# Second weights split one unit ahead, a pass edge's high parts before the weight splits, balancing sums in another bank: windowed attention and a Sinkhorn-balanced mixture of experts on one core

## The chip, the core and the metric

The program runs on one core of a Trainium2 chip. Its engines each work through a queue of their own in order: PE (matrix multiply, with PEld for its weight loads), DVE, ACT and POOL (elementwise), SP (which here issues the DMAs). Semaphores order the queues against each other. The metric is the device time of one execution in microseconds (us); lower is better.

## The reference, cut to what matters

```python
scores = scale * q @ k.T                     # batch 4, heads 8, seq 576, head_dim 64
scores = where(0 <= i - j < 64, scores, -1e9)
x = (softmax(scores) @ v) as [N=2304, D=512]
P = exp(x @ w_gate - max)                    # E = 8 experts
for _ in range(8):
    P /= P.sum(1, keepdims=True) + 1e-9
    P /= P.sum(0, keepdims=True) + 1e-9
    P *= N / E
out = sum_e P[:, e] * (relu(x @ w1[e]) @ w2[e])   # w1[e]: 512x1024, w2[e]: 1024x512
```

## The kernel before

**Numbers in two parts.** Every matrix operand is held as a high part (a cast to a shorter float, made by ACT) and a low part (what the cast lost, a subtraction by POOL or DVE). A product of two operands is three matmuls: high by high, high by low, low by high.

**Stage 1** (to about 206 us of the span) computes attention for 18 tiles of 128 rows, the gate, and the first half of expert 0's work. What later passes need goes to DRAM (`xd_r`, `xd_f`, `yd`).

**Stage 2** runs three passes over 6 row tiles each (`NPASS`, `TP`). A pass has 30 groups: a group is 256 of an expert's 1024 inner columns; expert 0 has two groups left, the others four. Two groups make a unit, so a pass has 15 units and stage 2 has 45; units are numbered u0 to u44 here. In a unit, `Group.run` is called for the even and the odd group: seven products of half size (a Strassen scheme) of 12 column blocks' worth of `x` parts `xc[0..6]` with first-weight parts `w1c`, into PSUM banks `a`, `b` and `c` (two buffers each), with ACT and DVE making the two parts `g` of the relu. Then `mm2(u, t)` for t = 0..5 multiplies `g` by the second weights' parts `w2c` (12 matmuls into a PSUM tile `yp`, two buffers), and DVE adds the tile into `acc`, scaled by the balanced probability. The first unit of an expert that opens a new sum has ACT work here too: `L252` scales `acc` (u3, u16, u31), or `L247` copies `yp` away (u1).

**Weights.** `fetch1(i)` and `fetch2(i)` load 512 KB of a group's first or second weights into one of three staging buffers `stg` (SP queue). `sums1` (POOL, 4 operations) makes the Strassen sums of the first weights; `split1` makes `w1c` (ACT casts at L143, POOL subtractions at L146); `split2` makes two `w2c` tiles (ACT casts at L155, POOL subtractions at L156). The ring of `w2c` has eight tiles, four per unit. Before the change `split2(s)` and `split2(s + 1)` stand in the same unit whose `mm2` reads them, at a hook (`extra(k)`) inside the even and the odd group.

**Balancing.** Eight Sinkhorn rounds run as `step()` after `mm2` tiles 0, 2 and 4 of u0 and u1 and 0 and 2 of u2: a matmul with the constant `part` gives column sums (L680) in a buffer of the ring `y`, the ring of `yp`, and DVE rescales `prob` (L682 to L684, L674 to L676). `sk_exp` before u0 puts the maximum in such a buffer and has ACT take the exponential (L670).

**Pass edges.** u14 and u29 end a pass. Shortly before, three units of each of the first two passes (u10 to u12, u25 to u27) load attention output for the next pass (`xd_f`) and form its four Strassen sums on POOL (`next_sums`, L266 to L269), behind the even group. In the edge unit `next_slot` reloads `xc[0..2]` by DMA and makes `xc[3..6]` from these sums: a cast on ACT (L707) and a subtraction on DVE (L708) after each of `mm2` tiles 0 to 3. `split1(s + 3)` stands after tile 1.

The order on every engine is the order of the code (`tc.manual_schedule`): no scheduler moves anything.

Of the kernel before, what the change touches and what calls it, by code (L numbers as in the profile page):

```python
# [11 lines left out]
ALU = mybir.AluOpType  # L12
# [9 lines left out]
def window_attention_sinkhorn_moe(ctx: ExitStack, tc: tile.TileContext, q, k, v, w_gate, w1, w2, out):  # L22
    nc = tc.nc
# [39 lines left out]
    xc = [big.tile([P, 2, 2, NB], F32R, name=f"xc{i}") for i in range(7)]  # L63
# [6 lines left out]
    def f32(ap):  # L70
        return ap.bitcast(F32)
# [33 lines left out]
    def fetch1(i):  # L105
        if i < len(groups):
            _, e, c = groups[i]
            stg = r_stg.new()
            nc.sync.dma_start(out=stg, in_=w1[e, :, c * 2 * P:(c + 1) * 2 * P].rearrange("(k p) f -> p k f", p=P))
            raw1[i] = stg  # L110

    def fetch2(i):
        if i < len(groups):
            _, e, c = groups[i]
            stg = r_stg.new().rearrange("p k f -> p (k f)").rearrange("p (c d) -> p c d", c=2)
            nc.sync.dma_start(out=stg, in_=w2[e, c * 2 * P:(c + 1) * 2 * P, :].rearrange("(c p) d -> p c d", p=P))
            raw2[i] = stg
# [14 lines left out]
    def split1(i):  # L132
        if i >= len(groups):
            return
        a, ws = raw1.pop(i), wsum.pop(i)
        w = r_w1.new()
        parts = [
            (slice(0, 2), a[:, 0:4, 0:P]),
            (slice(2, 3), a[:, 2:4, P:]),
            (slice(3, 7), ws.rearrange("p s k f -> p (s k) f")),  # L140
        ]
        for sl, src in parts:
            nc.scalar.copy(out=w[:, 0, sl].rearrange("p s k f -> p (s k) f"), in_=src)  # L143
        for sl, src in parts:
            o, h = (w[:, j, sl].rearrange("p s k f -> p (s k) f") for j in (1, 0))
            nc.gpsimd.tensor_tensor(out=o, in0=src, in1=f32(h), op=ALU.subtract)  # L146
        wt1[i] = w

    def split2(i):
        if i >= len(groups):  # L150
            return
        src = raw2.pop(i)
        for j in range(2):
            w = r_w2.new()
            nc.scalar.copy(out=w[:, 0], in_=src[:, j])  # L155
            nc.gpsimd.tensor_tensor(out=w[:, 1], in0=src[:, j], in1=f32(w[:, 0]), op=ALU.subtract)  # L156
            wt2[i, j] = w
# [4 lines left out]
    ps = {}  # L162
# [59 lines left out]
    side = {}  # L222
# [64 lines left out]
    with tc.manual_schedule():  # L287
# [348 lines left out]
        with ExitStack() as p2:  # L636
            ring_b = p2.enter_context(tc.tile_pool(name="ring_b", bufs=1, reuse_waits="tile"))
            sk_p = p2.enter_context(tc.tile_pool(name="sk", bufs=2, reuse_waits="tile"))
            ps_m = p2.enter_context(tc.tile_pool(name="ps_m", bufs=2, space=PSUM, reuse_waits="tile"))
            for nm in "abc":  # L640
                ps[nm] = lambda nm=nm: ps_m.tile([P, 512], F32, tag=f"q{nm}", name=f"q{nm}")[:, :NB]
            ps["y"] = lambda: ps_m.tile([P, 512], F32, tag="y", name="yp2")
            for r in rings.values():
                r.open(ring_b)

            def side_tile():
                return ring_b.tile([P, 4 * 2 * NB], F32, tag="side", name="side")

            side["acc"] = side_tile().rearrange("p (t d) -> p t d", t=TP)
            split1(1)  # L650
            fetch2(1)
            fetch1(2)


            pending = []
            state = {}

            def sk_tile(shape, name):
                n = 1
                for x in shape[1:]:  # L660
                    n *= x
                t = ps["y"]()[:shape[0], :n]
                return t.rearrange("p (t e) -> p t e", e=shape[2]) if len(shape) == 3 else t

            def sk_exp():
                mp = sk_tile([P, 1], "mb")
                nc.tensor.matmul(mp, lhsT=ones[0:1, :], rhs=max2, start=True, stop=True)
                nm = sk_p.tile([P, 1], F32, tag="nm", name="nm2", bufs=1)
                nc.vector.tensor_copy(out=nm, in_=mp)
                nc.scalar.activation(out=pv, in_=logit, func=AF.Exp, bias=nm)  # L670

            def sk_row():
                r = sk_p.tile([P, T], F32, tag="r", name="r")
                nc.vector.tensor_reduce(out=r, in_=prob[:, 0:T, :], axis=AX.X, op=ALU.add)  # L674
                nc.vector.reciprocal(out=r, in_=r)
                nc.vector.tensor_tensor(out=pv, in0=pv, in1=r[:, :, None].to_broadcast([P, T, E]), op=ALU.mult)  # L676

            def sk_col():
                cp = sk_tile([P, T + 1, E + 1], "cp")
                nc.tensor.matmul(cp, lhsT=part, rhs=prob, start=True, stop=True)  # L680
                c = sk_p.tile([P, E], F32, tag="c", name="c")
                nc.vector.tensor_reduce(out=c, in_=cp[:, :, 0:E].rearrange("p t e -> p e t"), axis=AX.X, op=ALU.add)  # L682
                nc.vector.reciprocal(out=c, in_=c)
                nc.vector.tensor_tensor(out=pv, in0=pv, in1=c[:, None, :].to_broadcast([P, T, E]), op=ALU.mult)  # L684

            sk_exp()
            sk_row()
            pending += [lambda: (sk_col(), sk_row())] * (ITERS - 1) + [sk_col]

            def step():  # L690
                if pending:
                    pending.pop(0)()


            def next_sums(p, j):
                if j == 0:
                    side["xt"] = side_tile().rearrange("p (i k n) -> p i k n", i=4, k=2)
                x = ring_b.tile([P, KD, 2 * P], F32, tag="xr2", name="xr2")
                nc.sync.dma_start(out=x, in_=xd_f[p - 1][j])
                x_sums(side["xt"][:, :, :, j * P:(j + 1) * P], x, nc.gpsimd)  # L700

            def next_slot(p, slot):
                if slot < 3:
                    nc.sync.dma_start(out=f32(xc[slot]), in_=xd_r[p - 1][:, slot])
                else:
                    src = side["xt"][:, slot - 3]
                    nc.scalar.copy(out=xc[slot][:, 0], in_=src)  # L707
                    nc.vector.tensor_tensor(out=xc[slot][:, 1], in0=src, in1=f32(xc[slot][:, 0]), op=ALU.subtract)  # L708

            n_units = len(groups) // 2  # L710
            per = n_units // NPASS
            for u in range(n_units):
                pas, at = divmod(u, per)
                more = pas + 1 < NPASS
                s = 2 * u

                def even(k):
                    if k == 1:
                        split2(s)
                        fetch1(s + 3)  # L720
                    elif k == 3 and more and per - 5 <= at < per - 5 + TP // 2:
                        next_sums(pas + 1, at - (per - 5))

                def odd(k):
                    if k == 0:
                        sums1(s + 2)
                        if more and at == per - 1:
                            next_slot(pas + 1, 0)
                    elif k == 1:
                        if more and at == per - 1:  # L730
                            next_slot(pas + 1, 1)
                        split2(s + 1)
                        fetch2(s + 2)
                    elif k == 3 and more and at == per - 1:
                        next_slot(pas + 1, 2)

                Group(s).run(even)
                Group(s + 1).run(odd)
                split1(s + 2)
                sums1(s + 3)  # L740
                fetch2(s + 3)
                for t in range(TP):
                    mm2(u, t)
                    if t % 2 == 0:
                        step()
                    if t == 1:
                        split1(s + 3)
                        fetch1(s + 4)
                    if more and at == per - 1 and t < 4:
                        next_slot(pas + 1, (4, 5, 3, 6)[t])  # L750


# [26 lines left out]
```

## Time and profile before

| what | value |
|---|---|
| median of 3 runs | 1677.88 us (1677.24 to 1678.26) |
| the profiled execution, its own time | 1677.76 us |
| its span, first to last instruction | 1676.0 us |
| busy: PE, PEld, POOL, DVE, ACT | 97%, 86%, 60%, 50%, 37% |
| mean granted PE clock | 0.989 |

PE is busy nearly throughout, so its busy share hides what matters: a matmul that runs at a lower clock or stands half issued counts as busy. Read the length of one unit instead. A unit is the stretch from one even group's first product to the next, and all 45 have the same matmuls (but for the eight small ones at L680), so any unit longer than the shortest kind has lost the difference to something. Then read, in that unit, what each engine was waiting for.

### The profile page before, as it was taken

To read this page: it belongs to the slowest core of one execution; us is meant where nothing else is said; L and a number is where in the kernel's file an instruction comes from. 1 tells how busy PE (TensorE), PEld (TensorE's weight loads), DVE (VectorE), ACT (ScalarE), POOL (GpSimd) and SP (SyncE) were. 2 spreads that over 40 slices of the span, in tenths; PEclk is the share of its full clock that TensorE was granted. 3 is DMA by queue.
4 is the path that set the end of the run, shared out by engine and by line. 5 is a ranking of instruction groups with operands and counts; after the bars stand their busy time and mean duration, and the time that the engine had idled before them with its cause. 6 is when DMAs were issued, how large, how long until landed. Compare 5 with 4: busy or idle time off the path is not lost.

```text
span 1676.0 us, 23815 instructions
## 1 busy us (share of the span) xinstructions
PE 1627.5 (97%) x9253; PEld 1440.0 (86%) x9253; DVE 833.5 (50%) x1411; ACT 622.3 (37%) x1267; POOL 1007.1 (60%) x942
## 2 busy tenths in 40 slices
PE   8999999999999889999999999999999999999999
PEld 6888888889889778898898898889888988988988
DVE  6666466555444434554454454334644544544543
ACT  5566434333323332334233233223333332332331
POOL 5245365656665667566666666665666666665662
PEclk9999999999999999999999999999999999999999
DMA  9766421222222112532212122221622221221221
GB/s 228 188 156 158 137 84 56 71 64 63 74 65 75 64 63 76 163 95 75 64 64 76 63 63 73 79 76 51 195 76 64 63 75 64 63 76 63 63 76 38
DMA packets 156624, 145.86 MB, mean 87 GB/s; under 512 B 62112, under 2 KB 123040, under 8 KB 156512
## 3 DMA queue, kind: packets, MB, share of 16 engines
q1 hardware_dynamic: 156512, 144.35, 29.2%
q8 instruction: 72, 1.18, 0.3%
q14 instruction: 40, 0.33, 0.1%
HBM read 121.65 MB, written 15.73 MB: 82 GB/s over the span
## 4 chain that ended last, share of the span: by engine, by line
PE 86%; POOL 6%; DVE 2%; DMA 2%; ACT 2%; issue 1%; SPq 0%; ACTq 0%; POOLq 0%; DVEq 0%
PE yp L235 41%; PE qb L175 15%; PE qa L175 11%; PE qc L175 9%; PE yp L519 3%; PE hp L505 3%; DMA xr<-xd_f 2%; POOL w1c L146 2%; POOL w2c L156 1%; PE vp L425 1%; PE sp L375 1%; PE tp L410 1%; PE tp L347 1%; POOL ws L126 1%; DMA q<-in_q_dram 1%
## 5 line engine op out<-in xcount | busy, mean ns | idle before, releaser
L235 PE MATMUL yp<-w2c,g 128*128 128x512 f32 x3240 | 764.7, 396 | 36.2 <-POOL w2c L156 23.2
L235 PEld LDWEIGHTS yp<-w2c,g 128*128 128x128 f32 x3240 | 615.6, 191 | 172.5 <-POOL w2c L156 28.1
L156 POOL TENSOR_TENSOR w2c<-stg,w2c 128x512 fp32r<-128x512 f32 x180 | 229.2, 1294 | 400.6 <-ACT w2c L155 400.6
L255 DVE SCALAR_TENSOR_TENSOR acc<-yp,prob,acc 128x512 f32<-128x512 f32 x240 | 180.0, 751 | 447.7 <-PE yp L235 434.6
L175 PE MATMUL qb<-xc,w1c 128*128 128x384 f32 x1620 | 327.5, 336 | 0.0
L175 PEld LDWEIGHTS qb<-xc,w1c 128*128 128x128 f32 x1620 | 283.2, 188 | 3.6
L146 POOL TENSOR_TENSOR w1c<-stg,w1c 128x512 fp32r<-128x512 f32 (+1 forms) x180 | 179.6, 1020 | 95.5 <-ACT w1c L143 95.5
L175 PE MATMUL qa<-xc,w1c 128*128 128x384 f32 x1080 | 222.3, 340 | 0.5 <-DVE ys L525 0.5
L146 POOL TENSOR_TENSOR w1c<-ws,w1c 128x1024 fp32r<-128x1024 f32 x90 | 218.4, 2427 | 0.0
L175 PE MATMUL qc<-xc,w1c 128*128 128x384 f32 x1080 | 216.4, 334 | 0.0
L175 PEld LDWEIGHTS qa<-xc,w1c 128*128 128x128 f32 x1080 | 188.8, 188 | 14.4 <-ACT p L195 10.4
L188 DVE TENSOR_TENSOR u<-qb,p 128x384 f32<-128x384 f32 x180 | 99.9, 555 | 199.9 <-PE qb L175 199.8
L175 PEld LDWEIGHTS qc<-xc,w1c 128*128 128x128 f32 x1080 | 190.5, 188 | 0.0
L143 ACT CAST w1c<-ws 128x1024 fp32r<-128x1024 f32 x90 | 94.6, 1051 | 256.4 <-POOL ws L129 256.4
L195 ACT COPY p<-qa 128x384 f32<-128x384 f32 x90 | 42.5, 472 | 329.4 <-PE qa L175 329.4
L180 ACT ACTIVATE g<-u 128x384 fp32r<-128x384 f32 x180 | 94.7, 526 | 172.6 <-DVE u L188 172.6
L185 DVE SCALAR_TENSOR_TENSOR g<-u,g 128x384 fp32r<-128x384 f32 x180 | 140.7, 782 | 8.3 <-ACT g L180 0.5
L155 ACT CAST w2c<-stg 128x512 fp32r<-128x512 f32 x180 | 102.0, 618 | 0.0
L188 DVE TENSOR_TENSOR u<-qc,u 128x384 f32<-128x384 f32 x180 | 99.8, 555 | 2.6
L180 ACT ACTIVATE g<-qa 128x384 fp32r<-128x384 f32 x90 | 44.2, 492 | 134.2 <-PE qa L175 134.2
L404 POOL TENSOR_TENSOR s<-s,rr 128x512 f32<-128x512 f32 x36 | 37.4, 1040 | 78.2 <-DVE rr L403 41.7
L143 ACT CAST w1c<-stg 128x512 fp32r<-128x512 f32 (+1 forms) x180 | 82.4, 505 | 0.0
(124 smaller groups left out, 1326.2 us busy)
## 6 DMA issues: line engine op xcount, KB each, us to landing
stg<-in_moe_w_dram SPq DMA_DIRECT2D x182, 512.0 KB, 3.5
xd_r<-xs SPq DMA_DIRECT2D x36, 128.0 KB, 2.9
xc<-xd_r SPq DMA_DIRECT2D x6, 768.0 KB, 5.8
out_dram<-acc SPq DMA_DIRECT2D x18, 256.0 KB, 3.1
vs<-v SPq DMA_DIRECT2D x35, 128.0 KB, 4.1
k<-in_k_dram SPq DMA_DIRECT2D x16, 256.0 KB, 4.7
q<-in_q_dram SPq DMA_DIRECT2D x16, 256.0 KB, 5.2
v<-in_v_dram SPq DMA_DIRECT2D x16, 256.0 KB, 4.4
```

What stands on the lines that cost most here:

```text
L143: nc.scalar.copy(out=w[:, 0, sl].rearrange("p s k f -> p (s k) f"), in_=src)
L146: nc.gpsimd.tensor_tensor(out=o, in0=src, in1=f32(h), op=ALU.subtract)
L155: nc.scalar.copy(out=w[:, 0], in_=src[:, j])
L156: nc.gpsimd.tensor_tensor(out=w[:, 1], in0=src[:, j], in1=f32(w[:, 0]), op=ALU.subtract)
L175: nc.tensor.matmul(bank, lhsT=w[:, a, ws, kk, :], rhs=xc[xs][:, b, kk, :], start=(first and j == 0), stop=(j == 5), skip_group_check=not f ...
L180: nc.scalar.activation(out=g[:, 0, :], in_=src, func=AF.Relu)
L185: nc.vector.scalar_tensor_tensor(out=g[:, 1, :], in0=src, scalar=0.0, in1=f32(g[:, 0, :]), op0=ALU.max, op1=ALU.subtract)
L188: nc.vector.tensor_tensor(out=dst, in0=bank, in1=src, op=ALU.add)
L235: nc.tensor.matmul(yp, lhsT=g[:, a, o:o + P], rhs=w[:, x, :], start=(i == 0), stop=(i == 11))
L255: nc.vector.scalar_tensor_tensor(out=at, in0=yp, scalar=pr, in1=at, op0=ALU.mult, op1=ALU.add)
L505: nc.tensor.matmul(hp, lhsT=w1s[c][:, a, kk, :], rhs=xs[j][:, b, kk, :], start=(i == 0), stop=(i == 3 * KD - 1))
L519: nc.tensor.matmul(yp, lhsT=g[:, a, o * P:(o + 1) * P], rhs=w[:, x, :], start=(i == 0), stop=(i == 11))
```

## The change

Four edits, all in stage 2. (1) `split2` runs for groups s + 2 and s + 3, those of the next unit, in the same hooks; `fetch2` moves ahead in step; at the start of stage 2 `split2(0)` and `split2(1)` are put before `sk_exp`. (2) In the edge unit the four ACT casts of `next_slot` come in a row, ahead of `split1(s + 2)`; the four DVE subtractions (`next_low`) stay one after each of tiles 0 to 3. (3) `split1(s + 3)` and `fetch1(s + 4)` come after tile 2, not tile 1. (4) The balancing sums use buffers of ring `c`, not `y`.

```diff
@@ start of stage 2
+            fetch2(1)
             split1(1)
-            fetch2(1)
+            split2(0)
+            split2(1)
+            fetch2(2)
+            fetch2(3)
             fetch1(2)
...
@@ sk_tile
-                t = ps["y"]()[:shape[0], :n]
+                t = ps["c"]()[:shape[0], :n]
...
@@ next_slot, for slots 3 to 6
-                    src = side["xt"][:, slot - 3]
-                    nc.scalar.copy(out=xc[slot][:, 0], in_=src)
-                    nc.vector.tensor_tensor(out=xc[slot][:, 1], in0=src, in1=f32(xc[slot][:, 0]), op=ALU.subtract)
+                    nc.scalar.copy(out=xc[slot][:, 0], in_=side["xt"][:, slot - 3])
+
+            def next_low(slot):
+                nc.vector.tensor_tensor(out=xc[slot][:, 1], in0=side["xt"][:, slot - 3], in1=f32(xc[slot][:, 0]), op=ALU.subtract)
...
@@ the loop over units
+                edge = more and at == per - 1
                 def even(k):
                     if k == 1:
-                        split2(s)
+                        split2(s + 2)
                         fetch1(s + 3)
...
                 def odd(k):
                     if k == 0:
                         sums1(s + 2)
...
                     elif k == 1:
-                        if more and at == per - 1:
-                            next_slot(pas + 1, 1)
-                        split2(s + 1)
-                        fetch2(s + 2)
+                        split2(s + 3)
+                        fetch2(s + 4)
+                    if edge and k in (0, 1, 3):
+                        next_slot(pas + 1, (0, 1, None, 2)[k])
...
+                order = (4, 5, 3, 6)
+                if edge:
+                    for slot in order:
+                        next_slot(pas + 1, slot)
                 split1(s + 2)
                 sums1(s + 3)
-                fetch2(s + 3)
+                fetch2(s + 5)
                 for t in range(TP):
                     mm2(u, t)
...
-                    if t == 1:
+                    if t == 2:
                         split1(s + 3)
                         fetch1(s + 4)
-                    if more and at == per - 1 and t < 4:
-                        next_slot(pas + 1, (4, 5, 3, 6)[t])
+                    if edge and t < 4:
+                        next_low(order[t])
```

**Unit u10, PE at the first two `mm2` tiles.** Before, PE reads the `w2c` that this unit's POOL queue makes:

```order
L175 MATMUL qc<-xc_83,w1c_5795 128x384 x6
L235 MATMUL yp_6034<-w2c_5888,g_2_5886 128x512 x3
L235 MATMUL yp_6034<-w2c_5891,g_3_5920 128x512 x3
L235 MATMUL yp_6034<-w2c_5974,g_4_5972 128x512 x3
L235 MATMUL yp_6034<-w2c_5977,g_5_6006 128x512 x3
```

POOL in the same unit before, with the odd group's `w2c_5974` and `w2c_5977` behind the sums for the next pass:

```order
L156 TENSOR_TENSOR w2c_5891<-stg_5713,w2c_5891 128x512
L266 TENSOR_TENSOR side<-xr_5935 128x2x128
L267 TENSOR_TENSOR side<-xr_5935 128x2x128
L268 TENSOR_TENSOR side<-xr_5935,side 128x2x128
L269 TENSOR_TENSOR side<-xr_5935,side 128x2x128
L126 TENSOR_TENSOR ws_5954<-stg_5802 128x256
L127 TENSOR_TENSOR ws_5954<-stg_5802 128x256
L128 TENSOR_TENSOR ws_5954<-ws_5954,stg_5802 128x256
L129 TENSOR_TENSOR ws_5954<-stg_5802,ws_5954 128x256
L156 TENSOR_TENSOR w2c_5974<-stg_5765,w2c_5974 128x512
L156 TENSOR_TENSOR w2c_5977<-stg_5765,w2c_5977 128x512
```

PE at the same place now:

```order
L175 MATMUL qc<-xc_83,w1c_5825 128x384 x6
L235 MATMUL yp_6050<-w2c_5644,g_2_5902 128x512 x3
L235 MATMUL yp_6050<-w2c_5647,g_3_5936 128x512 x3
L235 MATMUL yp_6050<-w2c_5723,g_4_5988 128x512 x3
L235 MATMUL yp_6050<-w2c_5726,g_5_6022 128x512 x3
```

POOL's order is unchanged, but its `w2c` there are numbers 5904 to 5993, read one unit later; PE now reads 5644 to 5726, made in u9.

**Start of stage 2, ACT.** `w2c` is cast from staging, `prob` is `sk_exp`'s, `p` is u0's first product on its way out of PSUM. Before:

```order
L143 CAST w1c_3152<-ws_2950 128x1024
L670 ACTIVATE prob<-logit,nm_3165 128x18x8
L195 COPY p_0_3175<-qa 128x384
L180 ACTIVATE g_4_3198<-qa 128x384
L155 CAST w2c_3200<-stg_2657 128x512
L155 CAST w2c_3203<-stg_2657 128x512
```

Now:

```order
L143 CAST w1c_3154<-ws_2950 128x1024
L155 CAST w2c_3161<-stg_2657 128x512
L155 CAST w2c_3164<-stg_2657 128x512
L155 CAST w2c_3167<-stg_3152 128x512
L155 CAST w2c_3170<-stg_3152 128x512
L674 ACTIVATE prob<-logit,nm_3181 128x18x8
L195 COPY p_0_3191<-qa 128x384
```

Four casts moved ahead of `prob` and `p`; the last two read `stg_3152`, which `fetch2(1)` fills.

**Pass edge, ACT behind the odd group of u14.** `xc` are the next pass's high parts. Before:

```order
L143 CAST w1c_7075<-ws_7006 128x1024
L707 CAST xc_85<-side 128x768
L143 CAST w1c_7123<-stg_6953 128x512
L143 CAST w1c_7123<-stg_6953 128x256
L143 CAST w1c_7123<-ws_7082 128x1024
L707 CAST xc_86<-side 128x768
L707 CAST xc_84<-side 128x768
L707 CAST xc_87<-side 128x768
```

Now:

```order
L710 CAST xc_85<-side 128x768
L710 CAST xc_86<-side 128x768
L710 CAST xc_84<-side 128x768
L710 CAST xc_87<-side 128x768
L143 CAST w1c_7095<-stg_6891 128x512
L143 CAST w1c_7095<-stg_6891 128x256
L143 CAST w1c_7095<-ws_7022 128x1024
L143 CAST w1c_7159<-stg_6969 128x512
```

All four casts moved ahead of both `split1`; three of them stood behind a cast that waits for POOL's `ws`.

## Rows read from the trace of the kernel before

**Rows 1.** The page's chain of waits: shares of the span by engine.
```profile
PE 86%; POOL 6%; DVE 2%; DMA 2%; ACT 2%; issue 1%; SPq 0%; ACTq 0%; POOLq 0%; DVEq 0%
```

**Rows 2.** Table by stretch: length, busy us of PE/PEld/DVE/ACT/POOL, clock, DMA share, GB/s.
```profile
207.12:241.56 34.44, 32.96 (x163) 29.05 (x164) 23.43 (x45) 11.10 (x21) 20.16 (x18) 1.00 0.31 100
241.56:276.67 35.11, 33.07 (x164) 28.98 (x162) 21.18 (x37) 13.40 (x25) 20.33 (x18) 1.00 0.17 60
276.67:310.13 33.46, 32.47 (x162) 28.66 (x160) 18.96 (x32) 11.27 (x21) 20.38 (x18) 1.00 0.19 63
310.13:345.64 35.51, 33.20 (x158) 28.94 (x157) 21.46 (x30) 14.38 (x26) 21.50 (x18) 0.95 0.20 60
345.64:376.90 31.26, 31.26 (x158) 28.07 (x157) 14.85 (x24) 10.69 (x20) 20.27 (x18) 1.00 0.22 68
533.23:644.50 111.27, 98.65 (x470) 87.12 (x469) 44.61 (x72) 32.62 (x60) 68.89 (x66) 0.95 0.22 71
675.76:709.98 34.22, 31.87 (x157) 27.91 (x156) 21.86 (x28) 13.63 (x24) 21.60 (x18) 1.00 0.54 173
741.24:773.55 32.31, 31.56 (x157) 27.99 (x156) 14.69 (x24) 14.39 (x26) 20.25 (x18) 1.00 0.21 65
1023.70:1135.28 111.58, 100.98 (x470) 88.90 (x469) 44.21 (x72) 32.62 (x60) 69.10 (x66) 0.92 0.22 71
1166.55:1202.04 35.49, 33.18 (x158) 29.11 (x157) 21.95 (x28) 13.62 (x24) 21.60 (x18) 0.95 0.55 173
1233.30:1265.78 32.48, 31.73 (x158) 27.91 (x157) 14.74 (x24) 14.38 (x26) 20.28 (x18) 1.00 0.21 66
```

**Rows 3.** Timeline of POOL and PE in u10: start, length, instruction [idle before, releaser].
```profile
545.96 0.74 POOL L266 TENSOR_TENSOR side<-xr 128x256 f32<-128x256 f32 x1 [5.76 <-DMA xr<-xd_f]
...
553.86 16.43 PE L235 MATMUL yp<-w2c,g 128*128 128x512 f32 x65 [4.20 <-POOL w2c L156]
...
564.25 2.41 POOL L146 TENSOR_TENSOR w1c<-ws,w1c 128x1024 fp32r<-128x1024 f32 x1
```

**Rows 4.** Table by stretch, the 3 us behind that wait of PE (columns as in rows 2).
```profile
553.86:556.86 3.00, 3.00 (x7) 2.30 (x8) 0.47 (x1) 0.62 (x2) 3.00 (x3) 0.50 0.16 42
```

**Rows 5.** Timeline of DVE in the edge unit u14.
```profile
694.60 3.15 DVE L708 TENSOR_TENSOR xc<-side,xc 128x768 fp32r<-128x768 f32 x1 [0.21 <-POOL w1c L146]
...
702.39 0.96 DVE L708 TENSOR_TENSOR xc<-side,xc 128x768 fp32r<-128x768 f32 x1 [3.99 <-ACT xc L707]
```

**Rows 6.** Timeline of ACT and PE in u3, an expert's first unit.
```profile
335.18 1.05 ACT L143 CAST w1c<-ws 128x1024 fp32r<-128x1024 f32 x1 [5.00 <-POOL ws L129]
336.14 2.55 ACT L252 ACTIVATE acc<-acc,prob 128x512 f32<-128x512 f32 x4
...
338.55 7.25 PE L235 MATMUL yp<-w2c,g 128*128 128x512 f32 x24 [2.31 <-DVE acc L255]
```

**Rows 7.** Timeline of PE and DVE in u0: a column sum, the tile behind it, a rescale.
```profile
224.68 0.45 PE L680 MATMUL yp<-prob,part 128*128 128x171 f32 x2
225.62 5.75 PE L235 MATMUL yp<-w2c,g 128*128 128x512 f32 x24 [0.49 <-DVE acc L242]
...
232.02 0.30 DVE L682 TENSOR_REDUCE c<-yp 128x8 f32<-128x152 f32 x1
...
233.90 2.43 DVE L676 TENSOR_TENSOR prob<-prob,r 128x144 f32<-128x144 f32 x1
```

**Rows 8.** Timeline of ACT and SP at the start of u0.
```profile
207.16 0.42 ACT L670 ACTIVATE prob<-logit,nm 128x144 f32<-128x144 f32 x1 [4.19 <-DVE nm L669]
207.47 0.43 SPq L116 DMA_DIRECT2D stg<-in_moe_w_dram  x1
208.47 0.48 ACT L195 COPY p<-qa 128x384 f32<-128x384 f32 x1 [0.88 <-PE qa L175]
...
210.93 1.13 ACT L155 CAST w2c<-stg 128x512 fp32r<-128x512 f32 x2
```

**Rows 9.** The page's DMA issues: KB each, median us from issue to landing.
```profile
stg<-in_moe_w_dram SPq DMA_DIRECT2D x182, 512.0 KB, 3.5
```

More of the change, by code (lines that the diff above doesn't have):

```diff
@@ L726, in odd @@
                         sums1(s + 2)
-                        if more and at == per - 1:
-                            next_slot(pas + 1, 0)
                     elif k == 1:
-                        if more and at == per - 1:
-                            next_slot(pas + 1, 1)
-                        split2(s + 1)
-                        fetch2(s + 2)
-                    elif k == 3 and more and at == per - 1:
-                        next_slot(pas + 1, 2)
+                        split2(s + 3)
+                        fetch2(s + 4)
+                    if edge and k in (0, 1, 3):
+                        next_slot(pas + 1, (0, 1, None, 2)[k])
                 Group(s).run(even)
                 Group(s + 1).run(odd)
+                order = (4, 5, 3, 6)
+                if edge:
+                    for slot in order:
+                        next_slot(pas + 1, slot)
                 split1(s + 2)
                 sums1(s + 3)
-                fetch2(s + 3)
+                fetch2(s + 5)
                 for t in range(TP):
```

## The prediction

> **What bounds the kernel now.** I read three views in this order. First the chain of waits: PE holds 86% of what ended last and POOL 6% [rows 1], so time can only be won where PE stands still or slow, and POOL is the first suspect. Second the table by stretch, cut at the first product of each unit [rows 2]. u4 is a unit in which nothing goes wrong: 31.26 us, PE busy for all of it, clock 1.00. I take that as the floor of a unit. The rows show what the long units lose against it: u0 3.18, u1 3.85, u2 2.20, u3 4.25, the three units u10 to u12 together 111.27 - 3 x 31.26 = 17.49, u25 to u27 together 111.58 - 93.78 = 17.80, the edge units u14 and u29 2.96 and 4.23, u16 1.05, u31 1.22. That is 58.2 us, and what the change can win in stage 2 is in this sum; the other units are at the floor within some tenths. Third, in each kind of long unit, the timeline with its releasers:
>
> - In u10, POOL sits 5.76 us before L266, waiting for the DMA of attention output, and everything queued behind it is late; PE waits 4.20 us for `w2c` of L156 [rows 3]. The 3 us behind that wait are run at a granted clock of 0.50, the lower level, 1.2 GHz [rows 4]; so a loss of 5.6 to 6.3 a unit is a wait of about 4 and half of the slow stretch behind it.
> - In the edge unit, DVE waits 3.99 us for ACT's `xc` cast [rows 5], which is queued behind `split1(s + 3)`; with DVE stand its `acc` additions, and PE for a free `yp`.
> - In u3, ACT waits 5.00 us for POOL's `ws` inside `split1(s + 3)` with four `L252` behind it, and PE waits 2.31 us for the `acc` of tile 2 [rows 6].
> - In u0, each column sum takes a buffer of `yp`'s ring, so PE waits 0.49 us for the tile just finished to be emptied [rows 7].
>
> **The change part by part.** The sum is made against the profiled execution's own 1677.76 us, which is 0.12 under the median, so nothing needs converting.
>
> *A, second weights a unit ahead.* No instruction is added in the loop: the same two casts and two subtractions stand at the same hooks for other groups, and POOL's order does not change. What changes is who waits: PE in u10 reads `w2c` made in u9. POOL still waits 5.76 us and its queue is still late; next late is `split1`, whose last subtraction ends at 564.25 + 2.41 = 566.66 [rows 3]. Without the stall the next unit starts at 533.23 + 31.26 = 564.5. But that last piece is for the odd group, which starts 7.3 us later (six tiles take about 16.6, as two take 5.75 [rows 7], and each group half of the rest), so 5 us are left. POOL is busy for 68.9 of the 93.8 us in three such units [rows 2], so its lateness does not add up. The eight `w2c` tiles are two units' worth, so the early writer finds its tiles already read. I take the whole loss back: -17.5 - 17.8 = **-35.3**. Bounds: nothing below the floor; at worst what remains is rival 3.
>
> *B, high parts first at the edge.* Four casts of 768 columns, by my estimate 0.85 us each since two of 512 take 1.13 [rows 8], come ahead of `split1(s + 2)`, so its work on ACT and POOL begins some 3 us later. In u10 `split1(s + 2)` has more than that in hand, since it is wanted only after all of `mm2`. DVE's subtractions now never wait for ACT, but each can still run into POOL: 3.15 us against 0.96 [rows 5]. Two such in four tiles of 2.8 us each leave `acc` in time, since `yp` has two buffers. Loss taken back: 2.96 + 4.23 = **-7.2**; bounds 0 and -7.2.
>
> *C, column sums in ring `c`.* u0 loses 3.18 in three steps and u2 2.20 in two, so a step costs 1.06 to 1.10 us of PE. The matmul itself stays; its row says 0.45, overlapping what stands before it by 0.1 or so [rows 7], and I keep 0.35. The wait of 0.49 and the restart behind it go. DVE's rescale stays: from 232.02 to 233.90 + 2.43 it takes 4.3 us in a bad case [rows 7]; two tiles give PE 5.75, so DVE keeps up. Eight steps by 0.73: **-5.8**; bounds -3 (DVE late once a unit) and -7.
>
> *D, `split1(s + 3)` one tile later.* ACT still stands 5 us for `ws`, but `L252` (or L247) of tile 2 is ahead of it. Behind it now is tile 3, whose `acc` is wanted by tile 5, one tile of 2.7 us later than before; the waits were 2.31 in u3 [rows 6] and less in the others. So u3, u16, u31 and what u1 loses beyond its three steps (3.85 - 3.2) nearly vanish: 4.05 + 1.05 + 1.22 + 0.6 = **-6.9**; bounds -3 and -7.1. It is close in u3: `acc` of tile 3 comes out some tenths before PE wants it.
>
> *E, the start of stage 2.* Here the change adds a wait. `split2(1)` stands on ACT ahead of `prob` and of `p`, and reads what `fetch2(1)` brings. SP issues that fetch at 207.47 [rows 8], behind the last store of stage 1 results, and writing it two lines earlier in the code does not move it past that store. A fetch of 512 KB takes 3.5 us in the median [rows 9], so the casts start at about 211.0, take 1.13 for two, then `prob` 0.42 [rows 8], and `p` starts at 212.5 where it started at 208.47. PE cannot accumulate product 2 into bank `a` before `p` is out, and DVE's first addition needs `p` too: PE stands for 4.0 us right in u0. Behind a wait of 4.20 PE ran 3 us at half clock [rows 4], which costs 1.5 more. So **+5.5**. Bounds: 0, if the fetch were issued as soon as its buffer is free, against which stands the store in front of it in a queue that goes in order; +8, with the fetch 1.3 us later and twice the slow stretch. I take the middle because every piece of it has a row. The POOL subtractions of these four `w2c` move with them; PE reads them only in `mm2`.
>
> *Nothing.* The SP queue keeps the same four fetches a unit, each behind one release; the reload of `xc[1]` falls behind one fetch, and has all of `mm2` to land before its use. The end of the kernel is untouched.
>
> Sum: -35.3 - 7.2 - 5.8 - 6.9 + 5.5 = -49.7, and 1677.8 - 49.7 = **1628.1**.
>
> **The rivals.**
> 1. *The start costs nothing.* The same sum without E: 1622.6. For it speaks that `fetch2(1)` is first in the code now; against it the time of its issue [rows 8].
> 2. *DVE and POOL block each other where the change counts on DVE.* The row of 3.15 us against 0.96 for the same subtraction, with POOL at work on `w1c` [rows 5], and 2.43 for a rescale of 144 columns [rows 7], are such waits. If they keep half of B, half of C's gain and half of D's, 3.6 + 2.9 + 3.4 stay: 1638. The Trainium skill, "SBUF — State Buffer", section "Who interferes with whom", has it as a rule: a DVE instruction with two SBUF inputs contends with a GpSimd instruction that reads SBUF. By that rule, with which the two rows agree, the four edge subtractions and the rescales still meet POOL after the change, since neither moved to another engine.
> 3. *POOL's lateness moves on to `split1`.* If the first weights were late by what the second were, half of A would stay: 1646. Against it the 5 us worked out above.
> 4. *Slower than before: the staging ring feeds lateness back.* All four fetches of a unit share three buffers and one SP queue, each waiting for POOL. If a fetch came after its reader in every unit, POOL would stand, release late, and delay the next. It decides once POOL's work and waits exceed the 31.26 us of a unit; it has 20.3 busy now [rows 2], so 11 us of new waits a unit would be needed, and 12.5 would put 1.2 us on each of 45 units: 1628 + 54 = 1682. Nothing in the rows points there.
> 5. *The change does not do what it says*, because `split2` waits for a `w2c` tile still in use: then A and the rest of POOL's order stay as they are, 1663. The count of eight tiles speaks against it.
>
> **How the numbers follow.** Forecast 0.70, rival 1 0.10, rival 2 0.13, rival 3 0.03, rival 4 0.02, rival 5 0.02. The range runs from 1621, rival 1 with C and D at their best ends, to 1640, rival 2 with E somewhat larger; it leaves out rivals 3 to 5 and some tails, not 2 in 10. Faster by over 0.2% (3.4 us, about what a measurement of this kernel can tell from no change): 0.96; within it 0.01; slower 0.03.
>
> **What would show it.** A: no wait of PE for L156 in u10 to u12, units of 31.3 at clock 1.00, while POOL's wait of 5.8 before L266 is still there. B: u14 and u29 at 31.3 to 32. C: u0 to u2 lose 0.35 a column sum. D: u3, u16, u31 under 31.6. E: `p` of u0 starting near 212.5 and u0 at about 38 us; if `p` starts before 210, rival 1 is right. If u14 and u3 stay over 33, rival 2 is. A unit after the first four over 31.6 everywhere would point to rival 4, and the forecast would be wrong.

## The result and the profile after

The changed kernel takes 1629.03 us in the median (1628.45 to 1629.75, 4 runs), beside 1677.79 us (1677.24 to 1678.26, 4 runs) of the kernel before on the same chip: a ratio of 0.971, 95% interval 0.9693 to 0.9727. The forecast was 1628.1. The span of the profiled execution went from 1676.0 to 1626.8 us, and the mean granted clock from 0.989 to 0.996.

The page's chain of waits of the changed kernel, against [rows 1]:

```profile
PE 96%; DVE 1%; DMA 1%; ACT 1%; issue 0%; SPq 0%; POOL 0%; ACTq 0%; POOLq 0%; DVEq 0%
```

POOL's 6% are gone, and DVE, DMA and ACT hold 1% each where they held 2%. The one transfer that still stands in the chain in stage 2 is 5.10 us at its start. The table by stretch of the changed kernel, cut at the first product of a unit as in [rows 2] (length, busy us of PE/PEld/DVE/ACT/POOL, clock, DMA share, GB/s):

```profile
207.62:246.82 39.20, 34.19 (x162) 30.64 (x163) 24.95 (x45) 12.06 (x23) 24.42 (x22) 0.91 0.36 115
246.82:279.08 32.26, 32.26 (x163) 28.92 (x162) 19.47 (x37) 13.41 (x25) 20.43 (x18) 1.00 0.21 66
279.08:311.03 31.95, 31.95 (x161) 28.64 (x160) 19.10 (x32) 11.28 (x21) 20.40 (x18) 1.00 0.21 66
311.03:342.78 31.75, 31.72 (x158) 27.83 (x156) 21.31 (x30) 14.38 (x26) 22.03 (x18) 1.00 0.21 67
530.38:623.84 93.46, 93.43 (x469) 84.41 (x468) 44.17 (x72) 32.66 (x60) 66.85 (x65) 1.00 0.25 79
655.12:686.40 31.28, 31.28 (x158) 28.06 (x156) 19.48 (x28) 13.63 (x24) 20.11 (x18) 1.00 0.47 152
998.84:1091.86 93.02, 93.02 (x470) 84.48 (x468) 44.43 (x72) 32.65 (x60) 67.62 (x66) 1.00 0.24 80
1123.11:1154.38 31.27, 31.27 (x157) 28.07 (x156) 19.47 (x28) 13.63 (x24) 20.09 (x18) 1.00 0.48 153
```

Row by row, these are the lengths and what became of each forecast:

| unit | before | after | change | forecast |
|---|---|---|---|---|
| u0 | 34.44 | 39.20 | +4.76 | +3.3 (E +5.5, three column sums -2.2) |
| u1 | 35.11 | 32.26 | -2.85 | -2.8 |
| u2 | 33.46 | 31.95 | -1.51 | -1.5 |
| u3 | 35.51 | 31.75 | -3.76 | -4.05 |
| u10 to u12 | 111.27 | 93.46 | -17.81 | -17.5 |
| u25 to u27 | 111.58 | 93.02 | -18.56 | -17.8 |
| u14, u29 | 34.22, 35.49 | 31.28, 31.27 | -2.94, -4.22 | -2.96, -4.23 |
| u16, u31 | 32.31, 32.48 | 31.27, 31.27 | -1.04, -1.21 | -1.05, -1.22 |

The changes sum to -49.1 us, and the span fell by 49.2. Every row but that of u0 came out within 0.8 us of its forecast; u0 is 1.5 longer. What holds it is at its start, on ACT, SP and PE of the changed kernel (start, length, instruction, and in brackets the idle time before and its releaser):

```profile
204.88 3.04 SPq L526 DMA_DIRECT2D yd<-ys  x2
208.01 3.25 SPq L116 DMA_DIRECT2D stg<-in_moe_w_dram  x3
213.13 1.14 ACT L155 CAST w2c<-stg 128x512 fp32r<-128x512 f32 x2 [8.61 <-DMA stg<-in_moe_w_dram]
214.49 0.46 ACT L195 COPY p<-qa 128x384 f32<-128x384 f32 x1
215.00 2.29 PE L175 MATMUL qa<-xc,w1c 128*128 128x384 f32 x6 [5.01 <-ACT p L195]
217.09 2.09 PE L175 MATMUL qb<-xc,w1c 128*128 128x384 f32 x6
```

The fetch is issued at 208.01, right behind the two stores of the first row; its first cast starts 5.12 us later, `p` follows at 214.49, and PE waits 5.01 us for it. Then two products take 2.29 and 2.09 us, where 1.20 is usual: half clock, 1.98 us more. Both together are 6.99 us.

### The profile page after: what moved, and what is told of

Same layout as the page of the kernel before. It is cut to its first block, busy times and chain, and to the rows that moved or that the text cites. A ratio compares the mean times of both kernels' runs of the same rounds, so it can differ in the third digit from the quotient of the medians.

```text
span 1626.8 us, 23899 instructions
## 1 busy us (share of the span) xinstructions
PE 1608.7 (99%) x9253; PEld 1432.6 (88%) x9253; DVE 828.4 (51%) x1411; ACT 623.1 (38%) x1267; POOL 1010.4 (62%) x942
## 4 chain that ended last, share of the span: by engine, by line
PE 96%; DVE 1%; DMA 1%; ACT 1%; issue 0%; SPq 0%; POOL 0%; ACTq 0%; POOLq 0%; DVEq 0%
PE yp L235 45%; PE qb L175 17%; PE qa L175 12%; PE qc L175 12%; PE yp L519 3%; PE hp L505 3%; PE vp L425 1%; PE sp L375 1%; PE tp L410 1%; PE tp L347 1%; DMA q<-in_q_dram 1%; ACT s L394 0%; DMA stg<-in_moe_w_dram 0%; DVE nm L382 0%; DVE s L379 0%
## 5 line engine op out<-in xcount | busy, mean ns | idle before, releaser
L235 PE MATMUL yp<-w2c,g 128*128 128x512 f32 x3240 | 746.6, 390 | 0.0
L235 PEld LDWEIGHTS yp<-w2c,g 128*128 128x128 f32 x3240 | 607.0, 188 | 125.0 <-DVE acc L255 0.9
```

The lines of the kernel that those rows point to most:

```text
L235: nc.tensor.matmul(yp, lhsT=g[:, a, o:o + P], rhs=w[:, x, :], start=(i == 0), stop=(i == 11))
```

## The experiments

All ratios are against the kernel before on the same chip. Edit numbers (1) to (4) are those of the change. Lengths of units come from one profiled execution of each kernel.

### What costs u0 its seven microseconds

**The fetch out of the queue.** One fetch is issued by ACT instead of SP; nothing else is changed from the changed kernel.

```diff
-            fetch2(1)
+            fetch2(1, nc.scalar)
```

> One edit on the changed kernel: fetch2(1) at the start of stage 2 is issued from ACT's DMA queue, where nothing of stage 1 stands in front of it, in place of SP's, where the last store of stage 1 does. My theory: the changed kernel loses about 7 us in u0 (39.20 against a floor of 31.26 and three column sums of about 0.32) only because ACT's casts wait for this fetch; issued near 201.5 it lands before 207, p starts near 209 and u0 takes 32.2 us, so 1622 us. Rival: the casts themselves and DVE behind them hold u0, or the weights come no sooner; then u0 stays over 36 and the time at 1626 or more.

Measured: 1621.96 us (1621.89 to 1622.75), ratio 0.9662 (0.9647 to 0.9676). u0 lasts 33.13 us. ACT of this kernel:

```profile
201.34 0.43 ACTq L116 DMA_DIRECT2D stg<-in_moe_w_dram  x1
...
204.90 1.14 ACT L155 CAST w2c<-stg 128x512 fp32r<-128x512 f32 x2 [0.17 <-DMA stg<-in_moe_w_dram]
...
208.95 0.48 ACT L195 COPY p<-qa 128x384 f32<-128x384 f32 x1 [0.89 <-PE qa L175]
...
213.53 1.14 ACT L155 CAST w2c<-stg 128x512 fp32r<-128x512 f32 x2 [1.94 <-DMA stg<-in_moe_w_dram]
```

The fetch leaves at 201.34, more than six us earlier; the casts are done before ACT's next work is ready, and `p` waits for PE alone. So the four extra casts in front of `p` cost nothing. The time is the 1622 that was expected, but u0 is 33.13 and not 32.2: of the 6.99 us that edit (1) costs it (39.20 against 32.21 without that edit, below), 6.07 were where the fetch stood in SP's queue. Of the other 0.92, the next experiment takes 0.62. The Trainium skill, "DMA: Bandwidth & Descriptors", section "Rules for kernel authors", says that spreading DMAs over the issuing engines does not help bandwidth, since all run on the same 16 DMA engines. This run does not speak against that: what it gained is order, a transfer that passes a store which the other queue was not ready to issue.

**The wait that is left.** On top of that, u0's `split2(2)` and `fetch1(3)` one hook later, because in the last row above ACT waits 1.94 us for a tile with a relu part queued behind it.

```diff
-                    if k == 1:
+                    if k == (1 if u else 2):
                         split2(s + 2)
                         fetch1(s + 3)
```

> The changed kernel with fetch2(1) on ACT's DMA queue, and in u0 alone split2(2) and fetch1(3) one hook later in the even group (hook 2, not 1). Theory: with fetch2(1) out of the way u0 lasts 33.13 us, and its largest remaining loss is a wait of ACT of 1.94 us for the staging tile of split2(2), with a relu part queued behind it. One hook later the tile has landed, and u0 falls to about 32.3: 1621.1 us. Rival: the relu part was not what PE wanted next, or POOL gets its two subtractions too late; then u0 stays within 0.3 of 33.1 and the time at 1622, or above.

Measured: 1621.58 us (1620.94 to 1621.84), ratio 0.9657 (0.9643 to 0.9672). u0 falls from 33.13 to 32.51, most of the 0.8 expected. In time the two kernels can't be told apart; they are the fastest ones of this study, some 7 us under the changed kernel.

**Why the fetch takes 5.1 us: the fetches behind it?** SP issues three fetches within 3.25 us there. A 2 KB transfer that reads the first one's tile holds the other two back until it has landed.

```diff
             fetch2(1)
+            hold = dram.tile([P, 4], F32, name="hold")
+            nc.sync.dma_start(out=hold, in_=raw2[1][:, 0, 0:4])
```

> On the changed kernel a DMA of 2 KB that reads what fetch2(1) brought stands on SP between it and the two fetches behind it, so these start only when it has landed. In the changed kernel it takes 5.1 us from issue to the first cast, where the median of such fetches was 3.5. My theory: the two fetches issued right behind it share its DMA engines and cost it some 1.3 us; held back, ACT's casts start about 3.8 us after the issue and u0 takes about 37.9 in place of 39.2 us: 1627.7. Rival: the extra time has another source (the store in front, the first touch of that memory), and the cast starts 5 us after the issue as before, u0 at 39.2.

Measured: 1628.63 us, ratio 0.970 (0.9685 to 0.9714). My theory fell. SP and ACT of this kernel:

```profile
207.89 0.39 SPq L116 DMA_DIRECT2D stg<-in_moe_w_dram  x1
...
213.62 0.90 SPq L116 DMA_DIRECT2D stg<-in_moe_w_dram  x2
...
213.17 1.14 ACT L155 CAST w2c<-stg 128x512 fp32r<-128x512 f32 x2 [8.77 <-DMA stg<-in_moe_w_dram]
```

With the later two held until 213.62, the first still takes 5.28 us from issue to cast.

**Or the store in front of it?** The last 256 KB store of stage 1 is cut to 8 KB, and the rest is written one tile earlier.

```diff
-                    nc.sync.dma_start(out=yd[t], in_=ys)
+                    if t == T - 1:
+                        nc.sync.dma_start(out=yd[t][:, 0:16], in_=ys[:, 0:16])
+                    else:
+                        nc.sync.dma_start(out=yd[t], in_=ys)
+                        if t == T - 2:
+                            nc.sync.dma_start(out=yd[T - 1][:, 16:], in_=ys[:, 16:])
```

> The changed kernel with the last store in front of fetch2(1) on the SP queue cut from 256 KB to 8 KB (16 of 512 columns of row tile 17's early result; the other columns of that tile get the rows of the tile before it, written earlier, so the first part of expert 0's output is wrong for those 128 rows). Theory: the store that is still under way on the same DMA engines is why fetch2(1) took 5.1 us from issue to landing where the median is 3.5; with it gone the first w2c cast of that fetch begins about 3.7 us behind the issue, u0 lasts about 37.8 us, and the time is 1627.6. Rival: the store has nothing to do with it (the fetch is slow for its place behind stage 1's other traffic or for itself); then 5.1 us, u0 at 39.2 and 1629.0 stay.

Measured: 1627.53 us (1627.22 to 1628.26), ratio 0.9694 (0.968 to 0.9709). SP, ACT and PE of this kernel:

```profile
207.37 2.19 SPq L116 DMA_DIRECT2D stg<-in_moe_w_dram  x3
...
211.43 1.14 ACT L155 CAST w2c<-stg 128x512 fp32r<-128x512 f32 x2 [7.54 <-DMA stg<-in_moe_w_dram]
...
213.30 2.29 PE L175 MATMUL qa<-xc,w1c 128*128 128x384 f32 x6 [3.94 <-ACT p L195]
215.39 2.22 PE L175 MATMUL qb<-xc,w1c 128*128 128x384 f32 x6
217.41 2.06 PE L175 MATMUL qc<-xc,w1c 128*128 128x384 f32 x6
```

From issue to cast it is now 4.06 us, 1.06 less, and PE's wait is 3.94 instead of 5.01. So with the store cut, 1.06 of the some 1.6 us by which the fetch was over its median are gone, and some 0.5 stays unexplained. The size is uncertain: in the other kernels here that leave this start alone, the same fetch behind the full store lands 4.7 to 5.2 us after its issue; with the small store it lands after 4.0. By that the store is worth 0.7 to 1.2 us. From ACT's queue, ahead of the store, the same fetch took 3.56 from issue to cast. But the time agrees with the expectation by accident: u0 lasts 39.23 us, not 37.8, because three products instead of two now run at half clock (1.09 + 1.02 + 0.86 = 2.97 over 1.20 each). Of the 1.2 us by which this span is shorter, 0.63 is u0 beginning earlier (206.99 against 207.62), and the six units u10 to u12 and u25 to u27 hold most of the rest. I did not follow either.

**The half clock behind the wait.** 14 small matmuls on a constant fill part of PE's wait in u0.

```diff
+            if self.i == 0:
+                warm = ps["y"]()
+                for _ in range(14):
+                    nc.tensor.matmul(warm[:, 0:P], lhsT=ones, rhs=ones, start=True, stop=True)
```

> On the changed kernel 14 small matmuls on constants, into an unused bank, stand between the second and the third product of u0's even group, where PE waits 5.0 us for p. They change nothing of what is computed. My theory: of the 7 us lost in u0, 5.0 are the wait and 2.0 the two products behind it, which ran at a granted clock of 0.50; with PE at work during the wait the clock stays at 1.00 and u0 takes 37.2 in place of 39.2 us: 1627. Rival: the slow products have another cause (data or DVE late), and they stay at over 2 us each.

Measured: 1628.78 us, ratio 0.9704 (0.9687 to 0.972). PE of this kernel:

```profile
209.86 3.29 PE L201 MATMUL yp<-ones 128*128 128x128 f32 x28
214.66 1.32 PE L175 MATMUL qa<-xc,w1c 128*128 128x384 f32 x6 [1.52 <-ACT p L195]
216.69 1.31 PE L175 MATMUL qb<-xc,w1c 128*128 128x384 f32 x6 [0.71 <-DVE u L188]
```

The slow products are gone (1.32 and 1.31 us), so the second term of the loss is the clock. But u0 only falls to 38.0, and not all of that is the clock: `p` is out 0.37 us earlier here, counted from the start of u0, and from the start of the first of the two products to that of the one behind them it is 0.84 less (3.18 us for 4.02). A faster PE then waits 0.71 us for DVE's first addition, which stands behind `prob`'s rescale, and in total the kernel can't be told from the changed one. Part of the slow stretch was covered by a wait that comes out as soon as it is gone.

### What each edit is worth

**Edit (1) alone**, on the kernel before: only the lines of `split2` and `fetch2`, with those at the start of stage 2.

```diff
-                        split2(s)
+                        split2(s + 2)
...
-                        split2(s + 1)
-                        fetch2(s + 2)
+                        split2(s + 3)
+                        fetch2(s + 4)
...
```

> The kernel before with edit 1 alone (second weights a unit ahead, with the casts in front of u0). If the parts add up as in the changed kernel's trace, it wins 36.4 in u10 to u12 and u25 to u27 and loses 7 in u0: 1677.8 - 29.4 = 1648.4; u14 and u29 keep 34.2 and 35.5, u3 35.5. Rival: the parts lean on each other (POOL late in u10 to u12 delays what edits 2 and 3 cleared), and the six units keep more than 1 us each over the floor: 1655 or more.

Measured: 1649.53 us, ratio 0.9825 (0.981 to 0.9841). u10 to u12 last 93.38 us and u25 to u27 93.01, as with all edits; u0 lasts 42.22. All of A and all of E belong to edit (1). One expectation missed: u14 did not keep 34.2 but lasts 35.47, as u29 does (35.49). PE waits as long in it as before (2.32 us), and the 3 us behind ran at a clock of 0.55, where they ran at 1.00 in the kernel before.

**Edits (2) to (4) without (1)**: the same lines put back in the changed kernel, with those at the start.

> The changed kernel with edit 1 undone (split2 in its own unit again, the start of stage 2 as before). It should lose the 36.4 us of u10 to u12 and u25 to u27 again and win back the 7 of u0: 1629.0 + 29.4 = 1658.4, with u10 to u12 together near 111.3. Rival: with split1(s + 3) one tile later PE's wait for w2c in those units is shorter or longer than before, and the six units differ by over 3 us in sum.

Measured: 1660.62 us, ratio 0.9892 (0.9877 to 0.9906). u0 lasts 32.21 us, so E is 39.20 - 32.21 = 6.99, the same as wait and slow stretch together. u10 to u12 take 112.69 and u25 to u27 112.72. PE in u10 of this kernel, and the table by stretch for what stands behind its wait:

```profile
543.28 17.68 PE L235 MATMUL yp<-w2c,g 128*128 128x512 f32 x65 [3.50 <-POOL w2c L156]
```

```profile
543.28:548.88 5.60, 5.60 (x13) 4.33 (x14) 0.75 (x1) 0.62 (x2) 5.52 (x5) 0.50 0.47 128
```

The old wait [rows 3] is back, and behind it the clock is 0.50 again [rows 4], so it is edit (1) that removes them. The wait is 0.70 shorter than before, but the slow stretch behind it is 5.60 us long, where it was 3.0 in u10 of the kernel before. So u10 is longer than it was (37.40 for 36.89), and the six units together come out 2.6 us above the kernel before, not level with it as expected.

**Edit (3) undone**: `split1(s + 3)` behind tile 1 again.

```diff
-                    if t == 2:
+                    if t == 1:
                         split1(s + 3)
```

> The changed kernel with edit 3 undone: split1(s + 3) and fetch1(s + 4) behind tile 1 again. By the sum, u3, u16, u31 and u1 lose what they lost before, 3.8 + 1.05 + 1.2 + 0.6 = 6.6: 1635.6, while the edge units u14 and u29 stay at 31.3, cleared by the four casts in a row. Rival: those units lost their time to the column sums and DVE's meetings with POOL, and stay under 32: 1629 to 1631.

Measured: 1633.64 us, ratio 0.973 (0.9714 to 0.9747). u3 lasts 34.10, u16 32.29, u31 32.34; u1 (32.26) and the edges (31.27, 31.26) lose nothing. In u3 PE waits as before, but its clock stays up. PE, and the 3 us behind its wait:

```profile
339.64 5.82 PE L235 MATMUL yp<-w2c,g 128*128 128x512 f32 x24 [2.27 <-DVE acc L255]
```

```profile
339.64:342.64 3.00, 3.00 (x13) 2.39 (x14) 2.90 (x3) 0.14 (x1) 1.33 (x1) 1.00 0.47 146
```

and the same 3 us in the kernel before, behind the wait of 2.31 us of [rows 6]:

```profile
338.55:341.55 3.00, 3.00 (x7) 2.42 (x8) 2.90 (x3) 0.14 (x1) 1.31 (x1) 0.50 0.46 159
```

The waits differ by 0.04 us, the clock is 1.00 in one and 0.50 in the other, and u3 is 34.10 in one and 35.51 in the other.

**Edit (4) undone**: the column sums in ring `y`.

```diff
-                t = ps["c"]()[:shape[0], :n]
+                t = ps["y"]()[:shape[0], :n]
```

> The changed kernel with edit 4 undone: the column sums in buffers of ring y again. By the sum each of the eight steps costs PE 1.08 in place of 0.33 us: u0, u1 and u2 get 2.2, 2.2 and 1.5 longer, 1629.0 + 5.9 = 1634.9. Rival: the steps are held by DVE's rescale, not by the buffer, and u1 and u2 stay near 32.3 and 32.0: 1629 to 1630.

Measured: 1634.76 us, ratio 0.9739 (0.9724 to 0.9754). u0, u1 and u2 are 2.48, 1.95 and 1.55 us longer, 5.98 in all.

**Edit (2) undone**: each cast of the edge in front of its own subtraction again.

```diff
-                if edge:
-                    for slot in order:
-                        next_slot(pas + 1, slot)
...
                     if edge and t < 4:
+                        next_slot(pas + 1, order[t])
                         next_low(order[t])
```

> The changed kernel with edit 2 undone: in the edge units the four ACT casts stand again one behind each of tiles 0 to 3, in front of their subtraction, while split1(s + 3) stays behind tile 2. The sum in the prediction gave this edit 7.2 us by itself: then u14 and u29 take 34.2 and 35.5 again and the time is 1636. Rival: split1(s + 3) behind tile 2 clears the edge without it, since only the cast after tile 2 then stands behind ACT's wait for ws, and the acc it holds up (tile 3) is wanted first by tile 5: u14 and u29 stay within 0.5 of 31.3 and the time at 1629 to 1630.

Measured: 1629.76 us, ratio 0.9709 (0.9694 to 0.9723): no difference from the changed kernel that this measurement shows. The theory fell, and the rival holds but for a tenth: u14 and u29 last 31.89 each, 0.6 more. DVE in u14 of this kernel:

```profile
673.26 3.14 DVE L713 TENSOR_TENSOR xc<-side,xc 128x768 fp32r<-128x768 f32 x1 [0.21 <-POOL w1c L146]
...
681.77 0.96 DVE L713 TENSOR_TENSOR xc<-side,xc 128x768 fp32r<-128x768 f32 x1 [2.60 <-ACT xc L710]
```

ACT's cast still comes late, but by 2.60 us where it was 3.99 [rows 5]: with edit (3) the second split stands one tile later, and two casts get ahead of it, where it was one.

**Edits (2) and (3) undone together**, to see whether either does the edge alone.

> The changed kernel with edits (2) and (3) both undone; (1) and (4) stay. Each undone alone cost 0.7 (edit 2) and 4.6 us (edit 3) over the changed kernel's 1629.0. If they are independent, both undone give 1629.0 + 0.7 + 4.6 = 1634.4 and the edge units u14 and u29 stay under 32.2. Theory: at the edge each of the two alone does the whole job, since either takes the high parts out from behind a split that waits for POOL; then with both gone the edges come back to 34.2 and 35.5, and the time is 1634.4 + 6 = about 1640.

Measured: 1641.01 us (1640.46 to 1644.88), ratio 0.978 (0.9763 to 0.9796). u14 and u29 last 34.20 and 35.47, as before the change (34.22, 35.49). DVE in u14 of this kernel:

```profile
684.36 0.96 DVE L713 TENSOR_TENSOR xc<-side,xc 128x768 fp32r<-128x768 f32 x1 [3.99 <-ACT xc L710]
```

This is the wait of [rows 5] again, to the hundredth. The two edits are not independent: one undone costs 0.7 us, the other 4.6, both 12.0 (medians from separate comparisons; the spans of the profiled executions give 0.9, 5.0 and 12.4). At the edge either takes nearly all of the 7.2 us.

## Why the prediction was right, point by point

**A, right (-36.4 for -35.3).** POOL and PE in u10 of the changed kernel:

```profile
542.45 0.74 POOL L266 TENSOR_TENSOR side<-xr 128x256 f32<-128x256 f32 x1 [4.93 <-DMA xr<-xd_f]
...
545.16 16.52 PE L235 MATMUL yp<-w2c,g 128*128 128x512 f32 x72
```

POOL's wait for the transfer is still there (4.93 us; 5.76 in [rows 3]), and PE runs all 72 matmuls of the unit without a break. The cause stayed and its reader moved away from it, as forecast. The six units even come out at 31.0 to 31.3: the "floor" of 31.26 was none. In u5, an undisturbed unit, 0.25 us are lost in the odd group. PE, ACT, DVE and POOL there in u5, and PE, ACT and DVE at the same place in u12:

```profile
380.96 0.74 POOL L126 TENSOR_TENSOR ws<-stg 128x256 f32<-128x256 f32 x1
381.00 1.11 DVE L185 SCALAR_TENSOR_TENSOR g<-u,g 128x384 fp32r<-128x384 f32 x1
383.05 0.46 ACT L195 COPY p<-qa 128x384 f32<-128x384 f32 x1
383.56 1.31 PE L175 MATMUL qa<-xc,w1c 128*128 128x384 f32 x6
...
599.80 0.55 DVE L185 SCALAR_TENSOR_TENSOR g<-u,g 128x384 fp32r<-128x384 f32 x1
601.46 0.48 ACT L195 COPY p<-qa 128x384 f32<-128x384 f32 x1
602.25 1.20 PE L175 MATMUL qa<-xc,w1c 128*128 128x384 f32 x6
```

In u5 POOL starts its sums 0.04 us ahead of DVE's `g`, which then takes 1.11 us instead of 0.55. All that follows is later: ACT copies `p` 9.02 us into the unit, against 8.63 in u12, and the second product of the odd group, which needs `p`, starts 1.15 us behind the one ahead of it instead of 1.04. The next two products lose 0.11 and 0.03 more. In u12 POOL still waits for its transfer at that time and disturbs nothing. So the meetings of DVE and POOL that rival 2 names are in the floor itself.

**B, right in its size, wrong in its cause.** The edges lost all 7.2 us. But the step "loss taken back" put that down to edit (2) alone. The runs show that (2) and (3) do the same work there: without (2) the edges are 0.6 longer each, without (3) not at all, without both they are back. The argument looked at one queue position and missed that the other edit moved the same blocking cast.

**C, right (-6.0 for -5.8).** Column sums now stand among the tiles of `mm2` with no wait. PE in u0 of the changed kernel, against [rows 7]:

```profile
232.18 0.45 PE L684 MATMUL qc<-prob,part 128*128 128x171 f32 x2
232.36 5.76 PE L235 MATMUL yp<-w2c,g 128*128 128x512 f32 x24
```

0.49 us of waiting and the restart are gone. What is left over the floor is 1.00 for three sums in u1 and 0.69 for two in u2, 0.33 to 0.35 each, which is the 0.35 that the forecast kept for the matmul.

**D, right in sum, in part for other reasons (-6.0 for -6.3 without u1).** u16 and u31 are as forecast. In u3 the forecast was -4.05 and -3.76 came; ACT, DVE and PE there in the changed kernel, against [rows 6]:

```profile
336.54 1.05 ACT L143 CAST w1c<-ws 128x1024 fp32r<-128x1024 f32 x1 [4.86 <-POOL ws L129]
337.50 1.94 ACT L252 ACTIVATE acc<-acc,prob 128x512 f32<-128x512 f32 x3
...
338.25 0.76 DVE L254 SCALAR_TENSOR_TENSOR acc<-side,prob,acc 128x512 f32<-128x512 f32 x1 [2.30 <-ACT acc L252]
339.11 0.75 DVE L255 SCALAR_TENSOR_TENSOR acc<-yp,prob,acc 128x512 f32<-128x512 f32 x1
...
325.92 17.02 PE L235 MATMUL yp<-w2c,g 128*128 128x512 f32 x72
```

ACT still stands 4.86 us and DVE 2.30 for what is queued behind it, but three `L252` are left instead of four, and PE has one more tile in hand. It is still held a little: the addition that frees the buffer for tile 5 ends at 339.86, and PE's weight loads stand 0.5 us for it. No matmul row shows the wait, but the 72 matmuls take 17.02 us where u10's take 16.52. That is the 0.49 that u3 keeps over the floor; D had this `acc` out some tenths before PE wants it. Undoing edit (3) gives back 2.35 of the 3.76; the other 1.41 is the half clock, which did not return with the wait. D counted it in without naming it. The 0.6 that D counted in u1 overlaps with C: u1 is at 32.26 with edit (3) undone, and without edit (4) at 34.21 against 35.11 before, so edit (3) takes 0.9 there by itself and nothing on top of edit (4).

**E, right in sign and mechanism, too small (+7.0 for +5.5).** The mis-sized term is the transfer, 3.5 us as the median of all fetches [rows 9]. This one took 5.1 from issue to cast. A median over 182 fetches was used for one that follows a 256 KB store by 0.4 us, although the trace of the kernel before has this very fetch. From the view of that one issue in the kernel before, at 207.47:

```profile
DMA to landing us min/median/max: 4.8/4.8/4.8
```

With 4.8 for 3.5 the same sum gives +6.8. The experiment with the small store puts up to 1.06 of the difference down to that store. The second term, 1.5 for half clock, measured 1.98. The upper bound of +8 covered both.

**The rivals.** Rival 1 (the start costs nothing, 1622.6) was wrong for this kernel, but it is what became of it once the fetch was in another queue: 1621.96. Rival 2 (1638) was wrong in its time. The blocking that it names exists: the same subtraction takes 3.14 and 0.96 us in the rows above. In the changed kernel the four of u14 take 0.95, 1.30, 1.65 and 1.04 us; the middle two meet this subtraction of POOL's, which itself takes 3.11 us where it took 2.41 in [rows 3]:

```profile
676.39 1.30 DVE L713 TENSOR_TENSOR xc<-side,xc 128x768 fp32r<-128x768 f32 x1
676.83 3.11 POOL L146 TENSOR_TENSOR w1c<-ws,w1c 128x1024 fp32r<-128x1024 f32 x1
679.11 1.65 DVE L713 TENSOR_TENSOR xc<-side,xc 128x768 fp32r<-128x768 f32 x1
```

With 0.75 for `acc` each is done inside the 2.7 us of a tile. The rule of the Trainium skill ("SBUF — State Buffer", "Who interferes with whom") that the prediction cites agrees with these rows. The meetings cost nothing where the engine has slack, as here, and 0.25 us where it has little, as in u5. Rival 3 (1646), rival 4 (1682) and rival 5 (1663) would have shown in u10 to u12 or in the units after u3; all are at 31.3 or less. The price of rival 4 does not follow from its own numbers: 20.3 busy and 12.5 of waits are 1.5 over 31.26, not 1.2, which makes 69 us and not 54.

**Where it could have gone wrong.** A and E both hang on edit (1), and the other edits were summed as if independent. By the spans of the profiled executions, (1) alone brings 27.1 us and (2) to (4) without it 17.0; that is 44.1, and all four together bring 49.2. Of the gap of 5.1, 2.6 are the six units u10 to u12 and u25 to u27, longer without edit (1) than in the kernel before; 1.3 are u14 with edit (1) alone, both with more of the half clock; and 0.8 are u0 there. In medians the gap is 2.3, which the intervals do not tell from none. Of the parts of the sum, B and D overlapped at the edge and C and D in u1, and there the sum took the loss once.

## What to carry to other kernels

When an engine is held up by a transfer that can't come earlier, let it work a unit ahead: the wait may stay if its reader no longer stands next to it. Price a transfer at the start of a stage by its own row, if the trace has it, and by what stands in front of it in its queue, not by the median of all, and give it another queue if it can pass there. Two edits that take the same blocking instruction out of the way are worth once what either is worth, so undo them together as well as singly.

## What the runs showed of the hardware that was not expected

The granted clock behind a short wait of PE is not set by the length of that wait. In the kernel before, PE waits 2.31 us in both edge units, u14 and u29, in the same code. Behind the wait, the two tiles that are left take 6.07 us in one and 7.36 in the other:

```profile
704.07 6.07 PE L235 MATMUL yp<-w2c,g 128*128 128x512 f32 x24 [2.31 <-DVE acc L255]
...
1194.84 7.36 PE L235 MATMUL yp<-w2c,g 128*128 128x512 f32 x24 [2.31 <-DVE acc L255]
```

The mean clock of the two units is 1.00 and 0.95 [rows 2]: this is the whole difference between their 34.22 and 35.49 us. In u3, 3 us ran at 0.50 behind a wait of 2.31 in the kernel before and of 2.27 with edit (1) alone, and at 1.00 behind a wait of 2.27 with edit (3) undone. After 5.01 us two products were slow, after 3.94 three. What decides was not found. A forecast can only count on either case, and where a row of one trace rests on it, some 1.3 to 1.4 us of that row are luck.

And two fetches of 512 KB issued right behind another did not delay it: 5.12 us with them, 5.28 with them held back.
